# A hand-written order of tasks in a fused attention and MLP kernel: the first 220 of 1230 tasks arranged anew

## The chip, the cores and the metric

The kernel runs on one core of a Trainium2 chip. A core has five instruction queues that run side by side and meet at semaphores: PE (TensorE, matmuls, with its weight loads shown as PEld), ACT (ScalarE), DVE (VectorE), POOL (GpSimd) and SP (SyncE, which here issues nearly all transfers). The metric is the device time of one execution in microseconds, median of the runs.

## The reference, cut to what matters

One transformer layer with 2048 tokens (S), width D = 512, 32 heads of 16, and an MLP of inner width 1376. A vector c gives scale, shift and gate for both halves. Attention is linear: queries and keys go through a small matrix per head and two softmaxes of 16, and keys are summed into one matrix per head.

```python
mod = (_silu(c) @ w_mod).reshape(c.shape[0], 6, 1, -1)      # sa, ca, ga, sb, cb, gb
h = _layernorm(x, axis=-1) * (1 + ca) + sa
x = x + ga * _A_ref(h, A_wqkv, A_w_phi, A_wo)
h = _layernorm(x, axis=-1) * (1 + cb) + sb
x = x + gb * _B_ref(h, B_w_gate, B_w_up, B_w_down)
...
pq = jnp.einsum('bhsd,hdf->bhsf', q, w_phi)                 # the same for k
phi_q = jnp.concatenate([_softmax(pq, axis=-1), _softmax(-pq, axis=-1)], axis=-1)
kv = jnp.einsum('bhsf,bhsd->bhfd', phi_k, v)
o = num / den                                               # phi_q @ kv over phi_q @ sum(phi_k)
...
h = _sigmoid(g) * u                                         # MLP: g, u = x @ w_gate, x @ w_up
```

## The kernel before

The 2048 tokens are 16 tiles of 128. All work is cut into 1230 named tasks. A task has a name, the engines that may run it (the first is the default), the keys that it reads and writes, and the buffers that it uses. The function `arrange` walks a string, `ORDER`, and emits the tasks in exactly this order; each engine runs its own tasks in the order in which they stand there. A letter behind @ picks the engine (A is ACT, D is DVE, P is POOL). Buffers (8 PSUM banks, 8 tiles xn, and so on) are handed out in the same walk, so a task also waits for whoever used its buffer last. Nothing is rearranged later, and no planner runs.

The tasks up to the key features of tile 4, by name (a number behind a name is the tile, or the tile group and the block j of 128 columns):

- `ld_...` on SP: loads. `ld_x0a` to `ld_x3a` bring x, `ld_wk0` and `ld_wk1` the key weights, `ld_wm00a` to `ld_wm01b` the first part of w_mod, `ld_wv0` the value weights, `ld_wmga` the gate's part of w_mod, `ld_wmm2` its last 1.5 MB (L556), `ld_wo` the output weights. `wqT0` to `wqT3` (L669) load a block of the query weights with a DMA that transposes.
- `wdz`, `warm0`, `warm1_0` to `warm1_11` (L600): matmuls on zeros into a spare bank.
- `c1`, `c2`, `c3`: silu of c. `modc1.0`, `modc1.1` (PE, L630) and `modc1c0`, `modc1c1` (L635, L638): scale and shift of the first layer norm. `modca`: the first gate. `modc2.0`, `modc2.1` (PE, L616) and `modc2c` (ACT, L643): the second layer norm's and the second gate; they read what `ld_wmm2` brings.
- `tpw`, `wTc`: transposes of the key weights on PE and their copies out of PSUM on ACT. `fold1j` and `fold0j` (PE, L679) multiply key and query weights by the small per-head matrix; `foldc` (ACT, L685) copies the result.
- `st1_t` (DVE, L702 and L703): mean and variance of a token tile. `rs1_g`: one over the root, of tile group g, on ACT (L709, L710) or POOL (L712, L713). `nmr1_g` (DVE, L718) and `xn1_t` (POOL, L731): the normalised tile. Groups 0 and 1 are tiles 0 and 1, group 2 is tiles 2 and 3, and so on in pairs up to group 8.
- `tphgj` (PE, L744) transposes xn; tiles 10 to 13 go by DMA instead (`xT1_t`, SP, L736). `hm1_gj` puts scale and shift on it, on ACT (L751), DVE or POOL (L753).
- `Kt`, `Vt`, `Qt` (PE, L817, L821, L871): keys, values and queries of tile t; a and b are their halves. `et`, `nt`, `rt`, `phit`: the two softmaxes of the keys (exp on ACT, L776; sums on DVE, L780; reciprocal on DVE or ACT, L794 and L795; product on DVE or POOL, L787). `qe`, `qn`, `qphi`: the same for queries. `va`: values copied out of PSUM. `kv` (PE, L282): the sum over tiles.

Behind these come the rest of keys and queries, `kvn` and `kvz` (DVE, L294 and L299), which close the sum over all tiles, `num` (PE, L326), the output projection, the second layer norm and the MLP, whose matmuls `g`, `u` and `y` take most of PE's time.

In SP's queue a load is issued only when the one eight issues earlier has landed, since eight completion semaphores are used in turn.

Of the kernel before, what the change touches and what calls it, by code (L numbers as in the profile page):

```python
# [43 lines left out]
modc1c1 st1_8 ld_x3a warm1_8 K1a hm1_23 xn1_5 xn1_4 tph12 nmr1_6 st1_9 hm1_03@A hm1_13@A hm1_02@A ld_wv0 wqT3 xn1_10 xn1_11 rs1_5@P K0a K0b tph31 hm1_42@A
warm1_9 hm1_12@A hm1_22@A tph32 e0.0 K3a tph30 K3b hm1_30@A ld_wmga K1b tph33 warm1_10 tph40 st1_14 st1_15 st1_13 hm1_31@A hm1_32 wqT0 e3.0 wqT1 K2b hm1_40
nmr1_5 rs1_8@P n0.0 nmr1_8 hm1_33 e2.0 V0a V1a fold03 xn1_9 xn1_8 V1b V0b e1.0 n2.0 V2a V2b tph50 hm1_50 warm1_11 xn1_15 xn1_14 n1.0 V3a wqT2 fold00 fold01
tph43 r0.0@A va1 va0 phi0.0 foldc03 fold02 foldc01 foldc02 n3.0 st1_12 foldc00 xT1_10 xT1_11 r2.0 va2@D ld_wmm2 modca.0 modca.1 hm1_60@P hm1_63@P hm1_62@P
tph82 hm1_82@A r3.0@A modcac r1.0@A phi2.0@D phi1.0@D V3b K4a K4b rs1_7@P Q0 Q2 kv0.0 Q1 qe0.0 va3 qe2.0 hm1_43@A qe1.0 modc2.0 tph52 modc2.1 tph51 nmr1_7
xn1_12 xn1_13 phi3.0@D ld_wo qn0.0 modc2c e4.0 kv1.0 qn2.0 hm1_52 kv2.0 Q4 K5a kv3.0 xT1_12 xT1_13 qphi0.0@P qphi0.1@P qn1.0 qe4.0 qphi2.1 tph80 K5b hm1_80@A
hm1_51@A e5.0 pT0 qphi2.0 n4.0 r4.0@A qn4.0 n5.0 phi4.0@D qphi1.1@P hm1_61@P qphi1.0@P tph53 V5 K7a V4 va5 hm1_53@A V6 pT2 hm1_70@P qphi4.1 va4 hm1_71 mask4  # L50
va6 K6a K7b K6b e6.0 K8 tph83 hm1_83 r5.0 qphi4.0@P e8.0 pT1 pT4 ld_wd2 tph81 hm1_81 n6.0 n8.0 e7.0 n7.0 V7 kv4.0 hm1_72@P K11 K9 V9 K14 V8 r6.0@A e9.0 va7
# [1007 lines left out]
```

## Time and profile before

| | |
|---|---|
| three runs | 205.24, 205.37, 207.14 us; median 205.37 |
| the profiled execution | span 203.3 us from the first to the last instruction; the execution's own time is not listed apart from it |
| busy share of the span | PE 96%, DVE 79%, ACT 52%, POOL 50% |
| chain that ended last | PE 75%, DVE 8%, ACT 4%, DMA 4%, issue 4%, POOL 3% |
| instructions | 4138, of them 1447 matmuls |
| transfers | 22.94 MB in 49453 packets |

The profile is one execution, seen by the hardware profiler. Times are microseconds from the start of the span. "Busy" counts an engine's own instructions; matmul ends are modelled. The chain of waits goes back from the last instruction, at each step to what released it. In timelines, a bracket at the end of a row is the idle time before that row and what ended it. Some matmul records are missing from a trace, so a count of x3 can stand for four.

### The profile page before, as it was taken

To read this page: it belongs to the slowest core of one execution; us is meant where nothing else is said; L and a number is where in the kernel's file an instruction comes from. 1 tells how busy PE (TensorE), PEld (TensorE's weight loads), DVE (VectorE), ACT (ScalarE), POOL (GpSimd) and SP (SyncE) were. 2 spreads that over 40 slices of the span, in tenths; PEclk is the share of its full clock that TensorE was granted. 3 is DMA by queue.
4 is the path that set the end of the run, shared out by engine and by line. 5 is a ranking of instruction groups with operands and counts; after the bars stand their busy time and mean duration, and the time that the engine had idled before them with its cause. 6 is when DMAs were issued, how large, how long until landed. Compare 5 with 4: busy or idle time off the path is not lost.

```text
span 203.3 us, 4138 instructions
## 1 busy us (share of the span) xinstructions
PE 194.9 (96%) x1447; PEld 106.7 (52%) x1471; DVE 160.6 (79%) x374; ACT 105.9 (52%) x257; POOL 102.1 (50%) x143
## 2 busy tenths in 40 slices
PE   7789999999999999999999999999999999999993
PEld 2455655555464687668844444444444444444442
DVE  3899999999999999999897797794969844326633
ACT  2799999999978984556451115212113311324100
POOL 4698977789689999767670056230030324000000
PEclk9999999999999999999999999999999999999999
DMA  5999975669952792417637224433112030100111
GB/s 172 331 329 182 233 264 102 123 82 280 400 213 43 146 102 55 94 37 106 125 59 103 51 54 103 101 83 77 26 26 69 13 79 31 40 13 7 50 55 55
DMA packets 49453, 22.94 MB, mean 113 GB/s; under 512 B 38065, under 2 KB 47634, under 8 KB 49426
## 3 DMA queue, kind: packets, MB, share of 16 engines
q1 hardware_dynamic: 48896, 22.59, 48.6%
q8 instruction: 13, 0.21, 0.4%
q14 instruction: 14, 0.11, 0.2%
q10 hardware_dynamic: 530, 0.02, 0.1%
HBM read 11.58 MB, written 2.10 MB: 67 GB/s over the span
## 4 chain that ended last, share of the span: by engine, by line
PE 75%; DVE 8%; ACT 4%; DMA 4%; issue 4%; POOL 3%; SPq 0%; POOLq 0%; DVEq 0%
PE y_ps L485 19%; PE u_ps L447 18%; PE g_ps L447 17%; PE a_ps L356 5%; DMA wmod_sb<-in_w_mod_dram 4%; PE k_ps L817 3%; PE warm L600 3%; DVE ks L780 3%; PE num L326 2%; POOL phi L787 2%; PE q_ps L871 2%; PE v_ps L821 2%; PE g_ps L449 1%; ACT h1T L751 1%; DVE qks L780 1%
## 5 line engine op out<-in xcount | busy, mean ns | idle before, releaser
L457 ACT ACTIVATE tg<-g_ps 128x512 bf16<-128x512 f32 (+5 forms) x66 | 28.8, 455 | 66.7 <-PE g_ps L447 39.5
L468 DVE SCALAR_TENSOR_TENSOR wmod_sb<-tg,u_ps 128x512 bf16<-128x512 bf16 (+4 forms) x63 | 30.3, 492 | 18.0 <-ACT tg L457 11.3
L485 PE MATMUL y_ps<-wd_sb,wmod_sb 128*128 128x512 bf16 (+4 forms) x180 | 44.2, 366 | 0.2
L447 PEld LDWEIGHTS <-wg_sb 128*128 128x128 bf16 (+1 forms) x252 | 21.9, 99 | 16.1 <-issue 0.2
L447 PEld LDWEIGHTS <-wu_sb 128*128 128x128 bf16 (+1 forms) x252 | 21.8, 99 | 16.0 <-issue 0.3
L784 POOL TENSOR_TENSOR qphi<-qe,qks 128x512 bf16<-128x512 bf16 x24 | 25.1, 1063 | 3.9 <-DMA pT<-qphi 1.0
L485 PEld LDWEIGHTS <-wmod_sb 128*128 128x128 bf16 (+1 forms) x187 | 17.1, 98 | 16.0 <-issue 0.6
L447 PE MATMUL u_ps<-wT_sb,wu_sb 128*128 128x512 bf16 (+2 forms) x124 | 23.8, 322 | 0.1
L447 PE MATMUL g_ps<-wT_sb,wg_sb 128*128 128x512 bf16 (+2 forms) x122 | 23.0, 321 | 0.2
L447 PE MATMUL g_ps<-wqk_sb,wg_sb 128*128 128x128 bf16 (+4 forms) x127 | 19.9, 286 | 0.1
L447 PE MATMUL u_ps<-wqk_sb,wu_sb 128*128 128x128 bf16 (+4 forms) x127 | 19.8, 286 | 0.2
L492 DVE TENSOR_TENSOR ot<-y_ps,x 128x512 bf16<-128x512 f32 (+2 forms) x17 | 11.1, 654 | 10.5 <-PE y_ps L485 10.4
L780 DVE TENSOR_REDUCE qks<-qe 128x64 bf16<-128x1024 bf16 x16 | 19.2, 1204 | 0.0
L780 DVE TENSOR_REDUCE ks<-e 128x64 f32<-128x1024 bf16 (+2 forms) x22 | 19.1, 905 | 0.0
L376 POOL TENSOR_SCALAR ve<-mv 128x2 f32<-128x2 f32 (+1 forms) x8 | 1.8, 226 | 34.2 <-DVE mv L366 34.1
L776 ACT ACTIVATE e<-k_ps 128x512 bf16<-128x512 f32 (+2 forms) x44 | 17.7, 504 | 0.1
L776 ACT ACTIVATE qe<-q_ps 128x512 bf16<-128x512 f32 x32 | 17.3, 608 | 0.8 <-POOL phi L787 0.4
L787 POOL TENSOR_TENSOR phi<-e,kr 128x1024 bf16<-128x1024 bf16 (+2 forms) x10 | 14.5, 1454 | 3.9 <-ACT kr L795 2.1
L817 PE MATMUL k_ps<-wqk_f,h1T 128*128 128x512 bf16 x61 | 15.9, 379 | 0.1
L356 PE MATMUL a_ps<-wo_sb,oT 128*128 128x512 bf16 x60 | 15.9, 379 | 0.2
L871 PE MATMUL q_ps<-wqk_f,h1T 128*128 128x512 bf16 x60 | 15.7, 379 | 0.2
L821 PE MATMUL v_ps<-wv_sb,h1T 128*128 128x512 bf16 x62 | 15.5, 379 | 0.0
(131 smaller groups left out, 306.4 us busy)
## 6 DMA issues: line engine op xcount, KB each, us to landing
out_dram<-ot SPq DMA_DIRECT2D x15, 128.0 KB, 1.8
x_sb<-in_A_x_dram SPq DMA_DIRECT2D x6, 256.0 KB, 4.9
wmod_sb<-in_w_mod_dram SPq DMA_DIRECT2D x1, 1536.0 KB, 7.4
wu_sb<-in_B_w_up_dram SPq DMA_DIRECT2D x1, 1376.0 KB, 11.0
wg_sb<-in_B_w_gate_dram SPq DMA_DIRECT2D x1, 1376.0 KB, 10.4
wd_sb<-in_B_w_down_dram SPq DMA_DIRECT2D x1, 1280.0 KB, 8.0
wmod_sb<-in_w_mod_dram SPq DMA_DIRECT2D x4, 256.0 KB, 6.0
wqk_sb<-in_A_wqkv_dram SPq DMA_DIRECT2D x2, 256.0 KB, 4.5
```

Source lines behind the costliest of these rows:

```text
L356: pe.matmul(ap_[:], lhsT=oT[:, j, :], rhs=wo_sb[:, j, :], start=(j == 0), stop=(j == KT - 1))
L447: pe.matmul(ps[:fsz, 0:n], lhsT=w[:, j, ft * P:ft * P + fsz], rhs=h[:, j, 0:n], start=(j == 0), stop=(j == KT - 1))
L457: G.add(f"tg{k}.{ft}", {"ACT": 0.13 + n * 0.00083}, lambda e, tg=tg, g_ps=g_ps, fsz=fsz, n=n: act.activation(tg[:fsz, 0:n], g_ps[:fsz, 0:n ...
L468: dve.scalar_tensor_tensor(hm_all[:fsz, hm[k].slot, ft, 0:n], tg[:fsz, 0:n], 1.0, u_ps[:fsz, 0:n], op0=ALU.add, op1=ALU.mult)
L485: mm = pe.matmul(y[:, 0:c1 - c0], lhsT=hm_all[:fsz, hm[k].slot, ft, tl * P:(tl + 1) * P], rhs=wd_sb[:fsz, ft, c0:c1], start=(ft == 0), sto ...
L776: act.activation(ee[:, a:b, s].rearrange("p g f h -> p g (f h)"), kp[:, a * 64:b * 64].rearrange("p (g n) -> p g n", n=64), ACT.Exp, scale ...
L780: dve.tensor_reduce(ks[:, a:b].rearrange("p g s h -> p (g s) h"), ee[:, a:b].rearrange("p g s f h -> p (g s) h f"), axis=AX.X, op=ALU.add)
L784: engine(e).tensor_tensor(ph[:].rearrange("p (g s f h) -> p g s f h", s=2, f=DH, h=4)[:, :, s], ee[:, :, s], ks[:, :, 1 - s].unsqueeze(2). ...
L787: engine(e).tensor_tensor(ph[:, a * P:b * P].rearrange("p (g f h) -> p g f h", f=DH, h=4), ee[:, a:b].rearrange("p g s f h -> p (g s) f h" ...
L817: pe.matmul(kp[:], lhsT=h1T[:, j, t * P:(t + 1) * P], rhs=wqk_f[:, j, D:2 * D], start=(j == 0), stop=(j == KT - 1))
L821: pe.matmul(vp[:], lhsT=h1T[:, j, t * P:(t + 1) * P], rhs=wv_sb[:, j, :], start=(j == 0), stop=(j == KT - 1))
L871: pe.matmul(qp[:], lhsT=h1T[:, j, t * P:(t + 1) * P], rhs=wqk_f[:, j, 0:D], start=(j == 0), stop=(j == KT - 1))
```

## The change

The string ORDER begins differently: its first 220 tasks, up to the point where `e4.0` (the exponentials of tile 4's keys) follows, stand in another order. They are the same 220 tasks, and six of them change engine: `rs1_0` and `rs1_4` from ACT to POOL, `hm1_21` and `r2.0` from DVE to ACT, `modc1c1` and `hm1_12` from ACT to DVE. The other 1010 tasks stand as they did. No function is touched.

```diff
 ORDER = """
-pmem ld_x0b wdz warm0 c1 warm1_0 warm1_1 bd st1_2 st1_3 warm1_2 warm1_3 c2 rs1_2 ld_x0a ld_wk0 warm1_4 tpw0 st1_0 rs1_0 wTc0 st1_1 ld_wk1 rs1_1 c3 xn1_0
...
+wdz warm0 c1 warm1_0 warm1_1 warm1_2 warm1_3 warm1_4 ld_x0b st1_3 st1_2 rs1_2 pmem ld_x0a c2 st1_1 ld_wk0 nmr1_2 tpw1 c3 rs1_1 ld_x1b wTc1 nmr1_1 st1_0 ld_wk1
...
```

What it moves is seen in the queues of the engines. First SP, from the load of x3a to ld_wmm2 (a line with + stands only in the new order, one with - only in the old; L537 is x, L551 wv, L669 a transposing load of query weights, L555 ld_wmga, L736 the two xT1, L556 ld_wmm2):

```order
+L669 DMA_TRANSPOSE wT_sb<-in_A_wqkv_dram 128x4x128
 L537 DMA x_sb<-in_A_x_dram 128x4x512
 L551 DMA wv_sb<-in_A_wqkv_dram 128x4x512
+L669 DMA_TRANSPOSE wT_sb<-in_A_wqkv_dram 128x4x128 x2
+L555 DMA wqk_sb<-in_w_mod_dram 128x4x512
 L669 DMA_TRANSPOSE wT_sb<-in_A_wqkv_dram 128x4x128
-L555 DMA wqk_sb<-in_w_mod_dram 128x4x512
-L669 DMA_TRANSPOSE wT_sb<-in_A_wqkv_dram 128x4x128 x3
 L736 DMA_TRANSPOSE h1T<-xn 128x4x128 x2
 L556 DMA wmod_sb<-in_w_mod_dram 128x4x1536
```

One transposing load has moved ahead of x3a, two stand ahead of ld_wmga instead of one, and one is left behind it instead of three; the set of issues ahead of ld_wmm2 is the same.

Next POOL, from `bd` to the tile that the first xT1 reads. Before (L731 is xn1, L712 and L713 together one rs1; the last row's x4 are tiles 5, 4, 10 and 11):

```order
L580 TENSOR_TENSOR bd<-wp_sb,bmask 128x4x64 x2
L731 TENSOR_SCALAR xn<-x_sb,rs_84,nmr 128x512 x5
L712 TENSOR_SCALAR ve_83<-mv_82 128x2
L713 TENSOR_TENSOR rs_84<-ve_83,mhalf 128x2
L712 TENSOR_SCALAR ve_83<-mv_82 128x2
L713 TENSOR_TENSOR rs_84<-ve_83,mhalf 128x2
L731 TENSOR_SCALAR xn<-x_sb,rs_84,nmr 128x512 x4
```

Now, from the rs1_0 that follows the first two xn1 (the x4 are tiles 7, 6, 5 and 4, the x3 tiles 11, 10 and 8):

```order
L713 TENSOR_TENSOR rs_84<-ve_83,mhalf 128x1
L731 TENSOR_SCALAR xn<-x_sb,rs_84,nmr 128x512
L712 TENSOR_SCALAR ve_83<-mv_82 128x2
L713 TENSOR_TENSOR rs_84<-ve_83,mhalf 128x2
L712 TENSOR_SCALAR ve_83<-mv_82 128x2
L713 TENSOR_TENSOR rs_84<-ve_83,mhalf 128x2
L731 TENSOR_SCALAR xn<-x_sb,rs_84,nmr 128x512 x4
L712 TENSOR_SCALAR ve_83<-mv_82 128x2
L713 TENSOR_TENSOR rs_84<-ve_83,mhalf 128x2
L712 TENSOR_SCALAR ve_83<-mv_82 128x2
L713 TENSOR_TENSOR rs_84<-ve_83,mhalf 128x2
L731 TENSOR_SCALAR xn<-x_sb,rs_84,nmr 128x512 x3
```

Ahead of tiles 10 and 11, which the xT1 read, stood nine xn1 in all with themselves and two rs1; now nine xn1 and five rs1 stand there.

Last DVE, around nmr1_6 (L718), which those two xn1 need. Before, from nmr1_3 on (L753 is hm1_23, the statistics are those of tile 8):

```order
L718 TENSOR_SCALAR nmr<-mv_82,rs_84 128x1 x2
L702 BN_STATS st_81<-x_sb 128x6
L703 BN_AGGR mv_82<-st_81 128x2
L753 TENSOR_SCALAR h1T<-tp_h,modc 128x256
L718 TENSOR_SCALAR nmr<-mv_82,rs_84 128x1 x2
```

Now, from modc1c1 on (L753 in turn: hm1_12, hm1_23, and as x2 hm1_40 and hm1_33):

```order
L638 TENSOR_TENSOR modc<-modc_ps,mone 128x2x2
L753 TENSOR_SCALAR h1T<-tp_h,modc 128x128
L753 TENSOR_SCALAR h1T<-tp_h,modc 128x256
L702 BN_STATS st_81<-x_sb 128x6
L703 BN_AGGR mv_82<-st_81 128x2
L702 BN_STATS st_81<-x_sb 128x6
L703 BN_AGGR mv_82<-st_81 128x2
L753 TENSOR_SCALAR h1T<-tp_h,modc 128x256 x2
L718 TENSOR_SCALAR nmr<-mv_82,rs_84 128x1 x2
```

nmr1_6 has moved behind modc1c1, hm1_12, the second of the statistics, hm1_40 and hm1_33; the two last read what PE's tph40 and tph33 write.

On PE, the new order puts tpw1, fold11 and the transposes tph10, tph12 and tph11 early, the warm matmuls warm1_5 to warm1_11 all ahead of tph21 (before, they stood singly between transposes and keys up to V3a), and tph52 ahead of modc2.0 instead of between modc2.0 and modc2.1.

More of the change, by code (lines that the diff above doesn't have):

```diff
@@ L44 @@
[L44 to L51, printed above, removed]
@@ new lines @@
+ld_x1a bd xn1_3 warm1_5 tpw0 wTc0 fold11 warm1_6 xn1_1 tpw2 foldc11 wTc2 st1_6 tph10 tph12 st1_7 tph11 ld_wm00b rs1_0@P tpw3 warm1_7 fold10 st1_5 xn1_2 wTc3
+tph13 fold12 warm1_8 warm1_9 ld_wm00a fold13 modc1.0 foldc10 foldc12 st1_4 rs1_4@P tph20 warm1_10 warm1_11 ld_x2b foldc13 modc1c0 hm1_11@A tph21 xn1_0
+hm1_10@A rs1_3@P tph02 tph01 ld_wm01b hm1_21@A ld_wm01a hm1_01@A nmr1_4 tph23 tph00 hm1_00@A st1_11 modc1.1 xn1_7 xn1_6 st1_10 nmr1_3 xn1_5 tph22 modc1c1@D
+K1a hm1_20@A ld_x2a hm1_12 hm1_02@A wqT1 ld_x3a tph03 xn1_4 hm1_23 hm1_13@A tph41 st1_8 hm1_03@A hm1_41@A st1_9 K0a hm1_22@A rs1_6@P tph43 hm1_43@A tph40 K1b
@@ new lines @@
+rs1_5@P K0b ld_wv0 wqT3 tph30 tph33 tph32 K2a tph42 hm1_40 wqT2 fold01 hm1_33 tph31 nmr1_6 K2b ld_wmga st1_14 hm1_30@A xn1_11 e0.0 hm1_31@A wqT0 xn1_10 xT1_11
+K3a xT1_10 K3b foldc01 nmr1_5 xn1_8 V3a st1_15 e3.0 V0a rs1_8@P e2.0 V0b V3b fold03 va3 foldc03 ld_wmm2 V2a st1_12 n0.0 V2b xn1_9 fold02 nmr1_8 r0.0@A hm1_32
+modca.0 va0 foldc02 modca.1 tph50 n2.0 xn1_15 modcac hm1_50 n3.0 e1.0 xn1_14 phi0.0 hm1_60@P V1a V1b hm1_62@P K4a hm1_63@P fold00 tph82 tph52 K4b foldc00
+r2.0@A va1 va2@D r3.0@A Q0 st1_13 rs1_7@P hm1_82@A n1.0 hm1_42@A kv0.0 Q2 Q1 r1.0@A phi3.0@D phi2.0@D modc2.0 qe0.0 modc2.1 nmr1_7 qe2.0 ld_wo xn1_12 phi1.0@D
```

76 lines of the change are left out of this document (38 added, 38 removed).

## The prediction

> **What bounds the kernel now.** I read the page first (busy shares and the 40 slices), then the windows of three stretches, the chain of waits in order of time, and last the timelines of PE (the matmul engine), SP (the queue that issues transfers), POOL, DVE and ACT in the first 60 us. The windows give, for each stretch, its length and the busy time of PE, weight load, DVE, ACT and POOL, then granted clock, DMA share and GB/s:
>
> ```profile
> 6.40:28.90 22.50, 20.11 (x194) 11.98 (x194) 21.45 (x60) 21.74 (x59) 18.30 (x29) 1.00 1.16 280
> 28.90:58.20 29.30, 29.09 (x284) 16.36 (x288) 28.49 (x51) 28.03 (x80) 23.26 (x22) 1.00 0.76 203
> 76.00:200.00 124.00, 123.26 (x766) 65.12 (x778) 90.13 (x203) 38.48 (x80) 39.57 (x56) 1.00 0.29 60
> ```
>
> PE is full (29.09 of 29.30, 123.26 of 124.00) from 28.9 us on, apart from short waits between 58 and 76. Whatever the front gains, PE must hand it on at 28.9. Before 28.9 PE idles 22.50 - 20.11 = 2.39 us: this is the only place where the changed tasks (they end at about 29 us) can save PE time. The chain of waits says what stands at 28.9 (start, length, what):
>
> ```profile
> 20.76 0.59 SPq L736
> 21.36 0.05 issue
> 21.41 7.44 DMA wmod_sb<-in_w_mod_dram
> 28.85 0.05 issue
> 28.90 0.82 PE modc_ps L616 x24
> ```
>
> The 1.5 MB load ld_wmm2 is issued at 21.41, lands at 28.85, and the matmuls of modc2.0 start at 28.90. In the timeline of PE the bracket at the end of a row is the idle time before it and what ended it:
>
> ```profile
> 8.92 0.62 PE L679 MATMUL fold_ps<-bd,wT_sb 128*128 128x128 bf16 x8 [0.94 <-ACT wT_sb L664]
> 28.90 0.82 PE L616 MATMUL modc_ps<-sc_bf,wmod_sb 128*128 128x1 bf16 x24 [0.22 <-DMA wmod_sb<-in_w_mod_dram]
> 29.58 0.27 PE L744 MATMUL tp_h<-ident,xn 128*128 128x128 bf16 x2
> 29.69 0.81 PE L616 MATMUL modc_ps<-sc_bf,wmod_sb 128*128 128x1 bf16 x24
> 58.57 0.93 PE L326 MATMUL num<-kvb,pT 128*128 128x68 bf16 x24 [0.36 <-DVE kvb L299]
> ```
>
> PE had come to modc2.0 only 0.22 us before the load landed. So two things meet at 28.9: PE's own work and one transfer. Whoever comes later sets the rest, since modc2.0 blocks all that is queued behind it on PE (kv1.0, kv2.0, Q4, K5a), and modc2c blocks ACT behind it (e4.0).
>
> **The change part by part.** Its size is the smaller of what PE and the transfer gain.
>
> PE's arrival. No matmul is added or removed; the order of 220 tasks changes. The largest hole, 0.94 us before fold11, came from ACT, which did rs1_0 and rs1_1 between the copies wTc. Now rs1_0 and rs1_4 run on POOL, tpw1 and wTc1 come first, and seven single warm matmuls (warm1_5 to warm1_11) stand in the early holes instead of among the transposes. If no idle time were left, PE would come to modc2.0 at 28.90 - 2.39 + 0.11 = 26.6 us; 0.11 is tph52, now ahead of modc2.0 (29.58 to 29.69 above). Some waits stay. The first copy wTc ran here on ACT:
>
> ```profile
> 6.89 0.59 ACT L664 COPY wT_sb<-tp_w 128x512 bf16<-128x512 bf16 x1 [0.24 <-PE tp_w L661]
> ```
>
> Now it is wTc1, and fold11 can't start before it ends at 7.48, while PE has only tpw1, one warm matmul and tpw0 before that: some 0.4 us idle. I allow 0.2 more for modc1.1, which needs its load and a PSUM bank from hm1_21. So about 27.2, and PE is 1.7 us early.
>
> ACT and DVE. The rows for the six changes of engine (start, length):
>
> ```profile
> 6.12 0.30 ACT L709 ACTIVATE ve<-mv,eps 128x1 f32<-128x1 f32 x1 [0.20 <-DVE mv L703]
> 6.45 0.20 ACT L710 ACTIVATE rs<-ve 128x1 f32<-128x1 f32 x1
> 12.19 2.42 ACT L751 ACTIVATE h1T<-tp_h,modc 128x128 bf16<-128x128 bf16 x6
> 14.48 0.18 ACT L635 COPY modc<-modc_ps 128x2 f32<-128x2 f32 x1
> 14.77 2.42 ACT L751 ACTIVATE h1T<-tp_h,modc 128x128 bf16<-128x128 bf16 x6
> 30.72 1.17 ACT L776 ACTIVATE e<-k_ps 128x512 bf16<-128x512 f32 x2
> 13.34 0.40 DVE L753 TENSOR_SCALAR h1T<-tp_h,modc 128x256 bf16<-128x256 bf16 x1
> 25.93 0.52 DVE L798 RECIPROCAL kr<-ks 128x64 bf16<-128x64 f32 x1
> ```
>
> ACT loses two rs1 (0.50 each by 0.30 + 0.20), modc1c1 (0.29 from 14.48 to 14.77) and hm1_12 (about 0.38, six from 12.19 to 14.48); it takes hm1_21 (0.38) and r2.0 (about 0.5). Net 1.0 + 0.29 + 0.38 - 0.38 - 0.5 = 0.8 us less. DVE loses hm1_21 (0.40) and r2.0 (0.52), takes hm1_12 and modc1c1 (at most 0.40 and 0.29): 0.2 us or more saved. Both are busy for nearly all of 6.4 to 28.9 (21.74 and 21.45 of 22.50), so they reach the end of the changed part some 0.6 us earlier. This is cover, not gain: e4.0 started at 30.72, behind modc2c, which needs modc2.1, which needs the load.
>
> The load. So the sum hangs on when ld_wmm2 lands. SP's timeline before:
>
> ```profile
> 9.42 1.01 SPq L551 DMA_DIRECT2D wv_sb<-in_A_wqkv_dram  x1
> 10.47 1.78 SPq L669 DMA_TRANSPOSE wT_sb<-in_A_wqkv_dram  x1
> 12.30 0.58 SPq L555 DMA_DIRECT2D wqk_sb<-in_w_mod_dram  x1
> 12.92 5.08 SPq L669 DMA_TRANSPOSE wT_sb<-in_A_wqkv_dram  x3
> 18.12 3.23 SPq L736 DMA_TRANSPOSE h1T<-xn  x2
> 21.41 0.57 SPq L556 DMA_DIRECT2D wmod_sb<-in_w_mod_dram  x1
> ```
>
> From 9.42 SP issues with hardly a gap up to 21.41, and the same 21 issues stand ahead of ld_wmm2 in both orders (15 loads, 4 wqT, xT1_10 and xT1_11). Only their order differs: wqT1 goes between x2a and x3a, wqT3 and wqT2 behind wv0, ld_wmga follows them, then wqT0, xT1_11, xT1_10. If each issue keeps its length, ld_wmm2 is issued at 21.4 and lands at 28.85. How the new order changes that no row shows, so I bound the shift.
>
> Earliest: the two xT1 need xn1_11 and xn1_10 from POOL.
>
> ```profile
> 5.24 1.50 POOL L580 TENSOR_TENSOR bd<-wp_sb,bmask 128x256 bf16<-128x256 bf16 x2 [2.13 <-DMA wp_sb<-in_A_w_phi_dram]
> 8.57 3.95 POOL L731 TENSOR_SCALAR xn<-x_sb,rs,nmr 128x512 bf16<-128x512 bf16 x5 [1.83 <-ACT rs L710]
> 14.54 3.03 POOL L731 TENSOR_SCALAR xn<-x_sb,rs,nmr 128x512 bf16<-128x512 bf16 x4
> 17.54 0.22 POOL L712 TENSOR_SCALAR ve<-mv 128x2 f32<-128x2 f32 x1
> 18.53 0.22 POOL L712 TENSOR_SCALAR ve<-mv 128x2 f32<-128x2 f32 x1
> ```
>
> Nine xn and two rs1 stood ahead, done at 14.54 + 3.03 = 17.57. Now nine xn and five rs1 do: three more at 18.53 - 17.54 = 0.99 are 2.97 us. But POOL can start its first xn when bd ends at 6.74, not at 8.57, if the statistics of tiles 3 and 2 come first (they do): 17.57 + 2.97 - 1.83 = 18.7. One issue of half 3.23 us after that, ld_wmm2 could go at 20.3, 1.1 us earlier.
>
> Latest: DMA throughput around transposes, from the windows of one us (last numbers: DMA share, GB/s):
>
> ```profile
> 17.00:18.00 1.00, 1.00 (x9) 0.54 (x7) 0.97 (x4) 1.00 (x3) 0.92 (x3) 1.00 1.15 349
> 18.00:19.00 1.00, 1.00 (x10) 0.56 (x8) 0.88 (x3) 1.00 (x4) 0.92 (x3) 1.00 2.93 103
> 19.00:20.00 1.00, 1.00 (x8) 0.44 (x5) 0.84 (x4) 1.00 (x4) 0.55 (x2) 1.00 0.27 52
> ```
>
> From 349 GB/s the queue falls to 103 and 52 where the transposes behind ld_wmga begin: (246 + 297) / 349 = 1.6 us of load time lost. The new order has three groups of transposes among the loads instead of two, so up to 1.6 us later.
>
> I take 0 between -1.1 and +1.6: the transfers ahead are the same ones, and the row of before (21.41) is the nearest. [...]
>
> Sum: landing 0, PE's work behind modc2.0 less tph52 -0.11, hence -0.1 us. PE then waits some 1.7 us instead of 0.22: its early gain is paid back at one point. The 0.36 us before num at 58.57 is DVE's; DVE's lead would cut it only if PE, which feeds it from 28.9 on, were earlier too. The profiled execution spans 203.3 us; the median of the runs is 205.37, so 2.1 us lie around the span, and they stay. 203.2 + 2.1, or 205.37 - 0.1: **205.3 us**.
>
> **The rivals.**
> A, the load comes early: with transposes spread among loads SP no longer issues five in a row (12.92 to 21.35 but for gaps), and POOL allows 1.1 us. For it: DMA fell to 52 GB/s while SP was still issuing. Against: each of SP's transposes was long exactly there, which a new order repeats. Midway, 0.7 earlier: 205.37 - 0.7 - 0.1 = 204.6; at the bound 204.2.
>
> B, slower: wqT1 between x2a and x3a costs its own dip in the queue, ld_wmga, wqT0 and the xT1 land later, and so does ld_wmm2; PE stands at L616 for longer. It decides from a landing after 28.96 (28.85 + 0.11). Middle of 0.4 to 1.6, 1.0 later: 205.37 + 1.0 - 0.1 = 206.3.
>
> C, slower by another way: nmr1_6 on DVE now stands behind hm1_40 and hm1_33, whose transposes tph40 and tph33 stand on PE behind K0a and K0b, which need ACT's hm1_03. POOL wants nmr1_6 for xn1_11 at 18.7 less two xn (3.03 / 4 = 0.76 each), 17.2. DVE's rows of one statistic:
>
> ```profile
> 15.34 0.68 DVE L702 BATCH_NORM_STATS2 st<-x_sb 128x6 f32<-128x512 bf16 x1
> 16.15 0.66 DVE L702 BATCH_NORM_STATS2 st<-x_sb 128x6 f32<-128x512 bf16 x1
> ```
>
> If modc1c1 starts at 13.6 (14.48 before, less ACT's lead of some 0.9), then with 0.29 for it, four hm1 at 0.40 and two statistics at 0.81 nmr1_6 starts at 17.1: just in time. What is late here goes one for one into xn1_11, both xT1 and ld_wmm2. At 0.8: 206.1.
>
> D, the clock: PE pauses at modc2.0. At the start the matmuls, though the granted clock reads full, ran at half the later rate:
>
> ```profile
> 1.24 2.74 PE L600 MATMUL warm<-wd_sb 128*128 128x512 bf16 x6 [1.24 <-DVE wd_sb L593]
> 36.21 2.32 PE L817 MATMUL k_ps<-wqk_f,h1T 128*128 128x512 bf16 x10
> ```
>
> 2.74 / 6 = 0.46 against 2.32 / 10 = 0.23 us each. If the pause of 1.7 us brought that state back for the 5.2 us that it lasted at the start (11 warm matmuls, 1.24 to tpw0), half would be lost: 2.6, total 207.9. The longest pause of before, 0.94 us, can't test it. [...]
>
> **How the numbers follow.** Forecast 0.47, A 0.22, B 0.20, C 0.07, D 0.04. The range 204.3 to 206.7 leaves out D, the far end of A (0.07) and of B and C (0.05): 0.16. One per cent, about what a measurement of this kernel can tell from no change, is 2.05 us: below 203.3 is only a load earlier than its bound (0.04); above 207.4 is D and a B worse than its bound (0.07); the rest, 0.89, is within.
>
> **What would show it.** In the changed profile: modc2.0 (L616, x24) waiting for DMA wmod_sb for 1 to 2 us; ld_wmm2 (L556) issued between 20.3 and 23.0 and landing near 28.9; the hole of 0.94 before fold11 gone; first xn on POOL near 6.8; PE full from there to num near 58.5. PE reaching modc2.0 after the load, or a landing off by over 1.6 us, would make the prediction wrong.

## The result and the profile after

| | before | changed |
|---|---|---|
| median of the runs | 205.39 us (204.68 to 207.56, 14 runs) | 203.90 us (203.60 to 204.34, 14 runs) |
| span of the profiled execution | 203.3 us | 202.3 us |
| runs with a mean granted clock under 0.995 | 23 of 35 (the runs beside e1, e2, e3 and e6 below) | 0 of 14 |

The ratio changed to before is 0.9911 [0.9888, 0.9934]: 0.9% faster, 1.5 us by the medians. In a second comparison (e7 below) the medians are 1.6 us apart, and the mean spans of the runs at full clock 1.4 us (203.33 and 201.97). The forecast was 205.3 with a range from 204.3; the result lies below it. The windows of the changed kernel over the same stretches (length, then busy time of PE, weight load, DVE, ACT and POOL, granted clock, DMA share, GB/s):

```profile
6.40:28.90 22.50, 20.84 (x244) 12.74 (x241) 21.31 (x60) 22.24 (x57) 20.97 (x33) 1.00 1.13 284
28.90:58.20 29.30, 28.77 (x261) 15.55 (x259) 29.05 (x57) 27.99 (x82) 24.04 (x23) 1.00 0.78 195
```

Before 28.9 PE now idles 22.50 - 20.84 = 1.66 us, where it idled 2.39. After 28.9 it idles 0.53 instead of 0.21: a little of the gain is given back. The chain of waits of the changed kernel, its pieces around ld_wmm2:

```profile
17.62 1.82 POOL xn L731 x3
20.52 6.87 DMA wmod_sb<-in_w_mod_dram
27.43 1.49 PE modc_ps L616 x48
```

The load is issued at 20.52 and lands at 27.39; before it was 21.41 and 28.85. The load is 1.46 us earlier, and modc2.0 starts 1.47 us earlier. The timeline of SP says how the issue came earlier (start, length); the two xT1 stand last, one by one, first those of before and then the changed kernel's:

```profile
8.72 1.50 SPq L669 DMA_TRANSPOSE wT_sb<-in_A_wqkv_dram  x1
11.44 2.95 SPq L669 DMA_TRANSPOSE wT_sb<-in_A_wqkv_dram  x2
15.06 1.57 SPq L669 DMA_TRANSPOSE wT_sb<-in_A_wqkv_dram  x1
17.96 2.50 SPq L736 DMA_TRANSPOSE h1T<-xn  x2
20.52 0.74 SPq L556 DMA_DIRECT2D wmod_sb<-in_w_mod_dram  x1
...
18.12 1.92 SPq L736 DMA_TRANSPOSE h1T<-xn  x1
20.14 1.22 SPq L736 DMA_TRANSPOSE h1T<-xn  x1
...
17.96 1.19 SPq L736 DMA_TRANSPOSE h1T<-xn  x1
19.25 1.21 SPq L736 DMA_TRANSPOSE h1T<-xn  x1
```

The same six transposing issues that took 1.78 + 5.08 + 3.23 = 10.09 us before now take 1.50 + 2.95 + 1.57 + 2.50 = 8.52. SP is done with the four wqT at 16.63 instead of 18.00, but then stands 1.33 us until POOL has written tile 11, so the first xT1 is issued only 0.16 us earlier (17.96 instead of 18.12). The other 0.73 us of the 0.89 are the pair of xT1 itself, 2.50 instead of 3.23. The rows of PE that matter, and one each of DVE, ACT and POOL:

```profile
7.31 0.40 PE L679 MATMUL fold_ps<-bd,wT_sb 128*128 128x128 bf16 x4 [0.44 <-ACT wT_sb L664]
12.66 0.55 PE L630 MATMUL modc_ps<-sc_bf,wmod_sb 128*128 128x1 bf16 x16 [0.56 <-DMA wmod_sb<-in_w_mod_dram]
24.30 1.02 PE L871 MATMUL q_ps<-wqk_f,h1T 128*128 128x512 bf16 x4 [0.36 <-ACT wqk_f L685]
27.43 1.49 PE L616 MATMUL modc_ps<-sc_bf,wmod_sb 128*128 128x1 bf16 x48
36.89 0.39 PE L744 MATMUL tp_h<-ident,xn 128*128 128x128 bf16 x4
37.45 1.02 PE L821 MATMUL v_ps<-wv_sb,h1T 128*128 128x512 bf16 x4 [0.17 <-ACT vaug L836]
57.51 0.93 PE L326 MATMUL num<-kvb,pT 128*128 128x68 bf16 x24 [0.36 <-DVE kvb L299]
...
28.00 0.33 DVE L718 TENSOR_SCALAR nmr<-mv,rs 128x1 f32<-128x1 f32 x2 [0.60 <-POOL rs L713]
...
29.93 1.18 ACT L776 ACTIVATE e<-k_ps 128x512 bf16<-128x512 f32 x2
...
17.17 2.27 POOL L731 TENSOR_SCALAR xn<-x_sb,rs,nmr 128x512 bf16<-128x512 bf16 x3
```

modc2.0 has no bracket (idle times under 0.15 us get none): PE and the load came together again, at 27.4. Behind it the V matmuls come at 37.45 where an unbroken PE would come at 37.12 (36.89 + 0.23, as 38.36 to 38.59 before): 0.33 us is lost there to ACT. In e7's profile, the same kernel once more, modc2.0 starts at 27.16, PE waits 0.22 us for DVE at 29.00, and the V matmuls come at 37.46, again behind ACT: the lead is not handed on in full. So num, 58.57 before, is 1.06 us earlier and not 1.47, and so is the end of the span (203.3 to 202.3).

### The profile page after: what moved, and what is told of

Its sections match the earlier page's. It is cut to its first block, busy times and chain, and to the rows that moved or that the text cites. A ratio compares the mean times of both kernels' runs of the same rounds, so it can differ in the third digit from the quotient of the medians.

```text
span 202.3 us, 4156 instructions
## 1 busy us (share of the span) xinstructions
PE 195.3 (97%) x1471; PEld 106.1 (52%) x1471; DVE 160.1 (79%) x374; ACT 105.1 (52%) x253; POOL 104.7 (52%) x147
## 4 chain that ended last, share of the span: by engine, by line
PE 74%; DVE 7%; DMA 6%; ACT 5%; SPq 3%; issue 2%; POOL 1%; POOLq 0%; DVEq 0%; ACTq 0%
PE y_ps L485 19%; PE u_ps L447 18%; PE g_ps L447 17%; DMA wmod_sb<-in_w_mod_dram 6%; PE a_ps L356 6%; PE k_ps L817 3%; PE v_ps L821 3%; PE num L326 2%; PE q_ps L871 2%; ACT e L776 2%; DVE ks L780 2%; PE g_ps L449 1%; DVE qks L780 1%; SPq L537 1%; DVE phi L787 1%
## 5 line engine op out<-in xcount | busy, mean ns | idle before, releaser
L457 ACT ACTIVATE tg<-g_ps 128x512 bf16<-128x512 f32 (+5 forms) x66 | 28.9, 455 | 66.8 <-PE g_ps L447 39.7
L485 PE MATMUL y_ps<-wd_sb,wmod_sb 128*128 128x512 bf16 (+4 forms) x187 | 45.7, 367 | 0.0
L817 PE MATMUL k_ps<-wqk_f,h1T 128*128 128x512 bf16 x64 | 16.6, 379 | 0.0
```

The costliest lines, as they stand in the source:

```text
L457: G.add(f"tg{k}.{ft}", {"ACT": 0.13 + n * 0.00083}, lambda e, tg=tg, g_ps=g_ps, fsz=fsz, n=n: act.activation(tg[:fsz, 0:n], g_ps[:fsz, 0:n ...
L485: mm = pe.matmul(y[:, 0:c1 - c0], lhsT=hm_all[:fsz, hm[k].slot, ft, tl * P:(tl + 1) * P], rhs=wd_sb[:fsz, ft, c0:c1], start=(ft == 0), sto ...
L817: pe.matmul(kp[:], lhsT=h1T[:, j, t * P:(t + 1) * P], rhs=wqk_f[:, j, D:2 * D], start=(j == 0), stop=(j == KT - 1))
```

## The experiments

In the edits a line with + or - names tasks of ORDER; the rest of the string is as in the kernel named. Each run lists its mean granted clock. One stretch of 3.41 us at half clock (0.50, as in e3's and e8's windows below) in a span of 203 us makes 1 - 3.41 x 0.5 / 203 = 0.992, two make 0.983. All runs fall near 0.983, near 0.991, or from 0.996 to 1.0; under 0.995 is called low.

| kernel | median us | ratio to before [95%] | low clock | mean span of the other runs |
|---|---|---|---|---|
| before, four comparisons | 205.37 to 205.74 | | 58 of 93 | 203.33 to 203.53 |
| changed (the result above; e7) | 203.90; 203.76 | 0.9911 [0.9888, 0.9934]; 0.9905 [0.9867, 0.9943] | 0 of 20 | 202.15; 201.97 |
| e1, changed, issue order of before | 204.69 | 0.9963 [0.9936, 0.9991] | 3 of 12 | 202.76 |
| e2, before, new issue order | 205.40 | 1.0000 [0.9972, 1.0027] | 10 of 12 | 202.90 |
| e3, changed, load ahead of the xT1 | 206.93 | 1.0058 [1.0029, 1.0086] | 7 of 12 | 204.52 |
| e6, changed, engines of before | 205.10 | 0.9963 [0.9938, 0.9988] | 3 of 12 | 203.23 |
| e8, changed without the seven warm | 205.25 | 0.9977 [0.9949, 1.0006] | 10 of 12 | 202.50 |
| e9, before, early warm | 205.42 (205.30 without its longest run, 207.85) | 0.9994 [0.9963, 1.0026] | 2 of 12 | 203.54 |
| e10, before, early warm and new issue order | 204.39 | 0.9933 [0.9906, 0.9960] | 2 of 12 | 202.57 |
| e5, changed, nmr1_7 later | 203.54 | 0.9878 [0.9839, 0.9917] | 1 of 7 | 201.68 |
| e11, changed, three moves | 204.43 | 0.9945 [0.9918, 0.9971] | 2 of 12 | 202.69 |
| e12, e5 and two more warm | 203.69 | 0.9919 [0.9893, 0.9945] | 0 of 8 | 202.01 |

**e1: the changed kernel with the issues in the old order.** The folds on PE are permuted so that each finds its block of weights.

```diff
 SP, from ld_x2a on
-ld_x2a wqT1 ld_x3a ld_wv0 wqT3 wqT2 ld_wmga wqT0 xT1_11 xT1_10 ld_wmm2 ld_wo
+ld_x2a ld_x3a ld_wv0 wqT3 ld_wmga wqT0 wqT1 wqT2 xT1_10 xT1_11 ld_wmm2 ld_wo
 PE (foldc on ACT likewise)
-fold01 ... V3b fold03 ... V2b fold02 ... tph50 ... fold00
+fold03 ... V3b        ... V2b fold00 ... tph50 fold01 ... fold02
```

> The changed kernel, with the twelve issues on SP from the load x2a to the load wo in the order of before (the three weight transposes wqT0, wqT1, wqT2 behind ld_wmga, wqT3 behind ld_wv0), and the four query folds on PE permuted so that each finds its transpose landed. Theory 1 (both needed: modc2.0 starts at the later of PE's arrival and the landing of ld_wmm2): ld_wmm2 is issued near 21.4 again and lands near 28.9, PE comes near 27.4 and waits about 1.5 us, and the time is 205.2, within 0.4. Theory 2 (the gain is PE's and ACT's earlier front alone): 203.9, as the changed kernel, even with such a wait. Theory 3 (the gain is the earlier load alone): 205.4, as before. Theories 1 and 3 part in the next run.

204.69: 0.8 to 0.9 us of the gain went, 0.7 stayed, so none of the three numbers. At full clock the spans say the same: 202.76 on average, 0.6 over the changed kernel's 202.15 and 0.8 under the 203.53 of before. The profiled execution had a stretch at half clock; e1b is a second profile of the same kernel.

> The kernel of run e1 (changed, with the issue order of before) once more, for a profile with the clock at 1.0 throughout, since e1's had a stretch at half clock. Theory 1 (modc2.0 starts at the later of PE's arrival and the load): ld_wmm2 issued near 21.3, landed near 28.6, PE at modc2.0 near 27.4 and waiting 1.2 us, and a span near 203.2, which leaves the 0.7 us by which e1 beat the kernel before unexplained. Rival: the load lands earlier here than in the kernel before, near 28.1, because something ahead of it on SP or in the queue is shorter, and the span is near 202.7.

Its span is 202.5. PE, SP and POOL there, at full clock throughout (POOL's x3 are tiles 11, 10 and 8):

```profile
28.30 1.50 PE L616 MATMUL modc_ps<-sc_bf,wmod_sb 128*128 128x1 bf16 x48 [0.49 <-DMA wmod_sb<-in_w_mod_dram]
...
12.91 5.09 SPq L669 DMA_TRANSPOSE wT_sb<-in_A_wqkv_dram  x3
18.62 2.70 SPq L736 DMA_TRANSPOSE h1T<-xn  x2
21.37 0.58 SPq L556 DMA_DIRECT2D wmod_sb<-in_w_mod_dram  x1
...
17.07 2.28 POOL L731 TENSOR_SCALAR xn<-x_sb,rs,nmr 128x512 bf16<-128x512 bf16 x3
```

With the old issue order the issue is back at 21.37 (21.41 before, 20.52 changed), and PE waits for the load, as theory 1 has it. But the load takes 28.25 - 21.37 = 6.88 us, as in the changed kernel (6.87) and not as before (7.44). The rival of e1b holds: of the 1.46 us by which the landing moved, 0.89 are the issue and go with the order of the twelve issues; 0.57 are the flight and do not. The 0.6 us that modc2.0 stays ahead of before (28.90 - 28.30) is most of what e1 keeps. Which part of the order gives the issue is seen in the rows: SP is done with the wqT at 18.00 and waits 0.62 us, since xT1_10, first in the old order, reads tile 10, which POOL writes second, at 18.59 (17.07 and two of 0.76). The pair of xT1 starts 0.66 us later than in the changed kernel and takes 0.20 longer. What the wqT spread among the loads give without the exchange of the two xT1 no run shows.

**e2: the kernel before with the new issue order only.** The edit is the first one of e1, in the other direction, on the kernel before.

> The kernel before, with only the twelve issues on SP from the load x2a to the load wo in the order of the changed kernel; PE, ACT, DVE and POOL as before. Theory 1 (both needed): ld_wmm2 is issued at 20.5 or earlier and lands by 27.4, PE comes at 28.7 as before and finds it there, so only the wait of 0.22 us goes: 205.2. Theory 2 (PE's front alone): 205.4. Theory 3 (the earlier load alone): 203.9.

205.40, no gain, as theories 1 and 2 have it within the interval; theory 3 (the earlier load alone) falls. In ten of twelve runs the clock was low, and then PE comes later still. In the profiled one PE reached L616 at 29.11, with the load issued at 19.93. The two runs at full clock span 202.8 and 203.0 us, under each of the twelve such runs of before beside them (203.1 to 204.6). So the earlier load alone probably gives some 0.6 us, which the clock hides in the median; two runs are few for it.

**e3: the load ahead of both xT1.**

```diff
 SP
-wqT0 xT1_11 xT1_10 ld_wmm2 ld_wo
+wqT0 ld_wmm2 xT1_11 xT1_10 ld_wo
```

> The changed kernel, with ld_wmm2 issued ahead of the two transposes xT1_11 and xT1_10, in the 1.33 us that SP waited there for POOL. Theory 1 (PE's own work now sets modc2.0 at 27.4): the load is issued near 16.7 and lands near 24, modc2.0 starts no earlier than 27.2, and the time is 203.8, within 0.3; both xT land later, behind the load, which may hold hm1_60 on POOL, and with it rs1_7, by up to 1 us and cost up to 0.5 us. Theory 3 (the load alone sets modc2.0): modc2.0 starts at 25 or earlier and the time is under 202.5.

206.93, slower. modc2.0 started at 27.36, so PE's own work sets it and the earlier load gains nothing; that part of theory 1 held. The price of the late xT1 was far over the 0.5 us allowed. POOL, DVE and PE of e3:

```profile
27.45 1.63 POOL L753 TENSOR_SCALAR h1T<-h1T,modc 128x256 bf16<-128x256 bf16 x3 [2.83 <-DMA h1T<-xn]
...
30.09 0.34 DVE L718 TENSOR_SCALAR nmr<-mv,rs 128x1 f32<-128x1 f32 x2 [2.60 <-POOL rs L713]
...
31.08 1.04 PE L282 MATMUL kvacc<-vaug,phi 128*128 128x68 bf16 x16 [2.08 <-DVE phi L787]
```

The 1.5 MB load, issued at 17.00, took 9.3 us to land (6.9 in the changed kernel), and of the two transposes issued behind it, from 18.02 on, one took 7.89 (the four of the changed kernel took 2.4 to 4.6). hm1_60 on POOL waited 2.83 us for them, rs1_7 behind it kept nmr1_7 on DVE for 2.60, phi1.0 stood behind that, and kv1.0 on PE for 2.08. Three engines, one late tile. At full clock the spans average 204.52, 2.4 us over the changed kernel. In the profiled execution the clock then halved, as e3's windows show:

```profile
27.76:31.17 3.41, 1.33 (x44) 1.16 (x42) 1.08 (x4) 2.71 (x9) 2.90 (x6) 1.00 0.18 53
31.17:34.59 3.42, 3.20 (x23) 1.77 (x24) 3.42 (x4) 1.70 (x4) 3.27 (x4) 0.50 0.32 61
```

**e6: the six changes of engine undone**, in the changed order.

```diff
-rs1_0@P rs1_4@P modc1c1@D hm1_12 hm1_21@A r2.0@A
+rs1_0 rs1_4 modc1c1 hm1_12@A hm1_21 r2.0
```

> The changed kernel's order with the six changes of engine undone (rs1_0, rs1_4, modc1c1 and hm1_12 on ACT; hm1_21 and r2.0 on DVE). Theory 1: ACT has 0.8 us more to do in the front and PE comes later by 0.3 to 0.8 us; POOL has two rs1 fewer, so xn1_11 and the load come earlier and PE's work alone sets modc2.0: 204.2 to 204.7. A rival, that the order alone did it and the engines' changes are cover: 203.9 or below.

205.10, worse than either theory. Among runs that are not low it is 203.23 - 202.06 = 1.2 us over the changed kernel (202.06 is the mean of its two means). So the changes of engine belong to the gain: this order needs them. How the 1.2 us come about at full clock stays open, since the profiled execution had half clock from 13.82 to 17.24. The load was not earlier there: it was issued at 22.13. DVE and SP of e6:

```profile
17.95 0.41 DVE L753 TENSOR_SCALAR h1T<-tp_h,modc 128x256 bf16<-128x256 bf16 x1 [1.02 <-PE tp_h L744]
18.27 0.33 DVE L718 TENSOR_SCALAR nmr<-mv,rs 128x1 f32<-128x1 f32 x2
...
15.04 1.58 SPq L669 DMA_TRANSPOSE wT_sb<-in_A_wqkv_dram  x1
19.57 2.50 SPq L736 DMA_TRANSPOSE h1T<-xn  x2
```

With PE at half clock its transposes come late, hm1_33 on DVE waits 1.02 us for them, nmr1_6 stands behind it (18.27; 16.34 in the changed kernel), POOL writes tile 11 late, and SP stands from 16.62 to 19.57. This is the chain that the prediction named as rival C. It is there in all five profiles of the changed front with half clock in this place: the first xT1 is issued at 19.96 in e1, 19.87 in e8, 19.20 in e5 and 19.48 in e11, against 17.96. PE itself is late too: in e6 the load lands at 28.91 and modc2.0 follows at 29.08 without a bracket.

**e7, e8: is the clock part of the gain?** e7 is the changed kernel itself, beside e8 to e10. e8 drops its seven single warm matmuls, whose results go nowhere.

```diff
-for i in range(12):  warm(f"warm1_{i}", ...)
+for i in range(5):   warm(f"warm1_{i}", ...)
 PE
-... warm1_5 ... warm1_6 ... warm1_7 ... warm1_8 warm1_9 ... warm1_10 warm1_11 ...
```

> The changed kernel as it is, beside the next three on one chip. The clock theory (the granted clock halves for a stretch of 3.4 us wherever a 3.4 us stretch before it holds too few streamed matmul columns; this happened in 23 of 35 runs of the kernel before in the first comparison and in none of 14 of the changed one): 203.9, a mean granted clock of 0.997 or more in at least 9 of 12 runs. Rival, that the granted clock depends on the chip and the hour: as many runs under 0.995 here as of the kernel before, and 204.5 or more.

> The changed kernel without the seven single warm matmuls warm1_5 to warm1_11 (their results go nowhere), so that the early holes on PE stay empty. The clock theory: most runs show a mean granted clock near 0.99, a stretch of 3.4 us at half clock between 9 and 17 us costs 0.8 to 1.7 us of PE's work, and PE comes to modc2.0 after the load: 204.8 to 205.4. Rival, that seven fillers in holes do nothing for the time: 203.7 to 204.0, and the clock stays at 1.0.

e7: 203.76, no low run of six, where 19 of 29 runs of before beside it are low. e8: 205.25, low in ten of twelve. The clock theory holds in both numbers: without the seven matmuls the median is 1.5 us longer. Its two runs at full clock span 202.4 and 202.6. e8's windows (the granted clock is the last column but two):

```profile
8.89:12.30 3.41, 2.33 (x37) 1.41 (x34) 3.27 (x11) 3.38 (x10) 2.89 (x7) 1.00 1.16 311
12.30:15.71 3.41, 2.91 (x28) 1.81 (x29) 3.27 (x11) 3.16 (x9) 3.33 (x6) 0.50 1.21 273
```

PE's timeline of e8 in the first of these windows, and ahead of modc2.0:

```profile
8.91 0.40 PE L679 MATMUL fold_ps<-bd,wT_sb 128*128 128x128 bf16 x4
9.47 0.40 PE L679 MATMUL fold_ps<-bd,wT_sb 128*128 128x128 bf16 x4 [0.16 <-ACT wT_sb L664]
10.27 0.55 PE L630 MATMUL modc_ps<-sc_bf,wmod_sb 128*128 128x1 bf16 x16 [0.40 <-DMA wmod_sb<-in_w_mod_dram]
10.68 0.38 PE L744 MATMUL tp_h<-ident,xn 128*128 128x128 bf16 x4
11.42 0.79 PE L744 MATMUL tp_h<-ident,xn 128*128 128x128 bf16 x5 [0.35 <-DVE xn L729]
...
28.18 1.89 PE L871 MATMUL q_ps<-wqk_f,h1T 128*128 128x512 bf16 x8
29.91 1.24 PE L616 MATMUL modc_ps<-sc_bf,wmod_sb 128*128 128x1 bf16 x40
```

Busy time does not part the stretches that half clock follows from the others: 2.33 us of PE here are followed by half clock, 2.12 us in one window of the kernel before were not. Columns do, in these profiles. Eight matmuls of 512 columns follow each other in 29.91 - 28.18 = 1.73 us, 0.42 ns a column. From 8.89 to 12.30 there are 17 matmuls of 128 columns and 16 of one: 17 x 128 x 0.42 ns = 0.92 us, 0.27 of the stretch. The same sum for every stretch of 3.41 us between 5 and 35 us, in the fourteen profiles. The stretches are counted in steps of the 3.41 us that half clock lasts, from the moments at which the trace notes a change of clock; that the steps run on where no change is noted is assumed (in the traces of before and of the changed kernel two changes lie 197.97 us apart, 58 steps of 3.413):

| share by columns (at full clock) | profile | the next 3.41 us |
|---|---|---|
| 0.06; 0.27; 0.32; 0.32; 0.33; 0.34; 0.37 | e3; e8; e2; e11; e5; e1; e6 | half clock, each |
| 0.41; 0.41; 0.41; 0.42; 0.42 | before (10.29); e3; e10; before (27.36); before (6.88) | full clock, each |
| 0.47; 0.48; 0.48; 0.48; 0.54 (the lowest of each) | changed; e7; e9; e12; e1b | full clock, each |

The border lies between 0.37 and 0.41 in these profiles; it is read from the same profiles, and no other measure of PE's work than busy time was compared. Stretches that are at half clock themselves are left out, and near the border they do not part clearly: e8's from 12.30 holds 0.38 by the same sum and is followed by half clock, e2's from 11.77 holds 0.35 to 0.39 (as matmuls on its edges are counted) and is followed by full. Where the 3.41 us begin differs between the profiles (a change is noted at 6.88 in the profile before, at 5.87 in the changed one). That the same kernel is low in only some of its runs for this reason is the author's estimate, from these profiles: with the steps slid along the profile before, at least one step between 3.5 and 30 us has under 0.39 for 77% of the possible beginnings (62% of its runs were low: 58 of 93). For the changed kernel it is 15% (none of 20), for e8 some 75 to 83% (10 of 12), for e2 some 75 to 86% (10 of 12), for e12 0 to 6% (none of 8), by where the border is put; for e6 it is some 48% (3 of 12). So it is a rough guide.

**e9, e10: the two parts put into the kernel before.** e9 moves its seven warm matmuls alone, e10 also the issues as in e2.

```diff
 PE
+warm1_5 warm1_6 warm1_7 (ahead of fold11)   warm1_8 (ahead of fold12)
+warm1_9 warm1_10 (behind modc1.0)           warm1_11 (ahead of modc1.1)
-warm1_5 to warm1_11 (behind tph22 and later)
```

> The kernel before, with the seven warm matmuls alone moved into the holes before fold11, before fold12 and around modc1.0 and modc1.1; every other engine and SP as before. The clock theory: the clock stays at 1.0 in most runs. Theory 1 (modc2.0 starts at the later of PE's arrival and the load): PE comes 0.9 us earlier (four of the matmuls stood where PE was full, 0.22 us each) and waits for the load, which lands near 28.8 as before: 205.1. Rival, that PE's front alone sets the time: 204.4.

> The kernel before, with the seven warm matmuls moved as in the run before and the twelve issues on SP in the changed kernel's order; ACT, DVE and POOL as before. Theory 1: the load lands near 27.4 or earlier, PE comes near 27.9, nothing waits: 204.3, so that these two parts give about 1.1 of the 1.5 us. Rival, that the six changes of engine and the new order of ACT, DVE and POOL are what gives the gain: 205.1.

205.42 and 204.39. By the medians neither part alone gives anything, both together 1.0 us. The two parts do two things, which the medians do not part: they bring PE and the load earlier, and they keep the clock up (2 of 12 runs low, against 19 of 29 of before beside them). At full clock alone the spans of e10 are 0.8 us under those of before (202.57 and 203.33), e9's 0.2 over. PE and the chain of waits of e9, then PE and SP of e10:

```profile
29.60 0.82 PE L616 MATMUL modc_ps<-sc_bf,wmod_sb 128*128 128x1 bf16 x24 [0.50 <-DMA wmod_sb<-in_w_mod_dram]
```

```profile
22.19 7.36 DMA wmod_sb<-in_w_mod_dram
```

```profile
28.24 0.82 PE L616 MATMUL modc_ps<-sc_bf,wmod_sb 128*128 128x1 bf16 x24
...
20.11 0.58 SPq L556 DMA_DIRECT2D wmod_sb<-in_w_mod_dram  x1
```

e9's clock is full and its PE early, but it waits for the load, which SP issues in the old order. (In this execution SP runs some 0.8 us behind the profile of before from its eleventh issue on, and the span is 204.3, where e9's full-clock runs average 203.54; so the size of the wait may be this execution's.) In e10 the load is issued 1.30 us earlier than before and no wait is left at modc2.0. By the trace's completion events it lands at 28.19, 8.08 us after its issue and later than the 27.4 expected, so PE and the load meet once more, at 28.2. The 0.6 us from e10 to the changed kernel (204.39 to 203.76) belong to the rest: the new order of ACT, DVE and POOL with the changes of engine, by which PE comes to modc2.0 at 27.43 and not at 28.24.

**e5, e11, e12: what is still to be had.** e5 takes away DVE's wait at nmr1_7; e11 adds two moves; e12 puts two more warm matmuls into the hole of 0.56 us ahead of modc1.1.

```diff
 e5
-nmr1_7 ... xn1_12 phi1.0@D
+phi1.0@D nmr1_7 xn1_12
 e11, and e5
-K4a fold00 (PE)   e1.0 foldc00 (ACT)   rs1_5@P xn1_11 xn1_10 xn1_8 (POOL)   nmr1_5 st1_15 (DVE)
+fold00 K4a        foldc00 e1.0         xn1_11 xn1_10 rs1_5@P xn1_8          st1_15 nmr1_5
 e12, and e5
+warm1_12 (PE, two matmuls, ahead of modc1.1)
```

> The changed kernel, with nmr1_7 on DVE moved behind phi1.0 (and xn1_12 on POOL with it in the list). In the changed kernel DVE waited 0.60 us at nmr1_7 for rs1_7 on POOL, with phi1.0 and all behind it queued, and PE gave back 0.33 us between 36.9 and 37.5, at the V matmuls that wait for ACT's vaug. Theory: DVE comes 0.5 us earlier to qn0.0, PE's loss there goes, and the time is 0.2 to 0.4 below the changed kernel's: 203.5. Rival, that ACT's own work sets vaug there and DVE's lead changes nothing: 203.85.

> The changed kernel with three moves: nmr1_7 as in the run before; V1a, V1b and fold00 ahead of K4a on PE and foldc00 ahead of e1.0 on ACT, so that Q0 no longer waits 0.36 us for foldc00; rs1_5 on POOL behind xn1_11 and xn1_10, with nmr1_5 and xn1_8 behind it, so that SP issues both xT1 and ld_wmm2 about 0.5 us earlier. Theory 1 (PE's arrival and the load both set modc2.0, now both near 27.0): 0.4 less at modc2.0 and 0.3 less at V5: 203.2. Rival, that one of the two moves fails to bring its side earlier (the load by its place in the queue, or PE by a wait of K4a): 203.5, as the run before.

> The kernel of run e5 with one more warm task of two matmuls (results go nowhere) ahead of modc1.1 on PE, in the hole of 0.56 us in which PE waits for the load of wm01. In e5's profile the stretch of 3.41 us ahead of the half-clock stretch held matmuls for 0.33 of its time by columns, and no stretch with 0.41 or more was followed by half clock in any profile so far; two matmuls of 0.215 us raise it to 0.45. The clock theory: no run has a mean granted clock under 0.995 (e5: one of 7), and DVE's wait at nmr1_7 is gone as in e5: 203.5 or 0.1 less, PE without idle time at the V matmuls near 37.5. Rival, that the clock falls with single idle gaps and not with what a stretch of 3.41 us holds: one or two of 12 runs fall as before.

e5: 203.54, and 0.3 to 0.5 us under the changed kernel in the spans of the runs that are not low. The two were not timed side by side, and e12, which has the same move, averages 202.01 at full clock, as the changed kernel does (202.15 and 201.97). So a gain in time is not shown. That the wait itself goes is seen in e12, which has the same move and a profile at full clock. DVE and PE of e12 (its line numbers from 605 on are one higher):

```profile
27.90 0.34 DVE L719 TENSOR_SCALAR nmr<-mv,rs 128x1 f32<-128x1 f32 x2
...
36.80 0.39 PE L745 MATMUL tp_h<-ident,xn 128*128 128x128 bf16 x4
37.03 0.81 PE L822 MATMUL v_ps<-wv_sb,h1T 128*128 128x512 bf16 x3
57.01 0.93 PE L326 MATMUL num<-kvb,pT 128*128 128x68 bf16 x24 [0.36 <-DVE kvb L299]
```

nmr1_7 waits no more, the V matmuls follow 0.23 us after the transposes, and num comes at 57.01, 0.50 us before the changed kernel's, though modc2.0 starts at 27.4 in both. e12's median, 203.69, is not below e5's. The clock was full in all its eight runs; e5 had one low run in seven, too few to tell the two apart.

e11: 204.43, a miss. With rs1_5 moved back on POOL, DVE and PE wait, as two rows of e11 show:

```profile
21.21 0.33 DVE L718 TENSOR_SCALAR nmr<-mv,rs 128x1 f32<-128x1 f32 x2 [1.19 <-POOL rs L713]
...
24.17 0.23 PE L744 MATMUL tp_h<-ident,xn 128*128 128x128 bf16 x1 [0.54 <-POOL xn L731]
```

This execution had half clock from 13.42 to 16.84, and with such a stretch SP issued the first xT1 at 19.20 to 19.96 in e1, e5, e6 and e8 too, without this move, so how much of these waits is the move's is not shown. At full clock e11's spans average 202.69, 1.0 us over e5's.

## Why the prediction was wrong

The step that failed is the load: "I take 0 between -1.1 and +1.6: the transfers ahead are the same ones, and the row of before (21.41) is the nearest." It was -1.46 us, beyond even the lower bound: -0.89 from the issue, which the sum took to keep its lengths, and -0.57 from the flight, for which the sum had no term.

- **The issue.** "If each issue keeps its length, ld_wmm2 is issued at 21.4." The lengths did not keep: six transposing issues went from 10.09 to 8.52 us. Read one issue at a time, the trace of before shows that the lengths differ: the row of 5.08 us is 2.46, 1.27 and 1.26, and the pair of xT1 is 1.92 and 1.22. In the two profiles each wqT right behind a load took 1.50 to 2.46 us and each behind another wqT 1.26 or 1.27; but the first xT1 of before took 1.92 behind a wqT, so the place behind a load is not the whole of it. What came through is the pair of xT1 (0.73 us); the wqT's 1.37 us met POOL's tile 11 and gave 0.16. So the bound from POOL, 20.3, was nearly met (20.52). e1 and e1b show that the order of the twelve issues does it, the exchange of the two xT1 included: put back, it gives 21.37 again.
- **The flight.** It was taken to stay at 7.44 us; it was 6.87. e1b has 6.88 with the old order of the twelve issues, so that order is not what shortened it. In all nine profiles with the changed front and the load in its old place (changed, e1, e1b, e5 to e8, e11, e12) it is 6.58 to 7.03 us, in the four with the order of before on ACT, DVE and POOL (before, e2, e9, e10) 7.13 to 8.08. So it goes with the rest of the new order; how is open.
- **PE's arrival.** "About 27.2": modc2.0 started at 27.43 without a bracket, right. The hole before fold11 was 0.44 (some 0.4 foretold); the one before modc1.1 was 0.56, for which 0.2 was allowed. Since PE was early, the load's shift came through in full, where the forecast had PE wait 1.7 us.
- **ACT and DVE.** ACT's 0.8 us held: e4.0 came at 29.93 instead of 30.72. DVE's lead was eaten by the wait of 0.60 us at nmr1_7, so qn0.0 came only 0.10 us earlier (28.85), and PE lost 0.33 us at 37.45. The step "cover, not gain" held only while the load was late: once modc2.0 came 1.47 us earlier, ACT's side set the V matmuls (37.45) and the gain at num was 1.06. In e12's profile that loss is gone with the wait.
- **POOL.** Tile 10 was to be ready at 18.7; the second of three xn from 17.17, at 0.76 each, put it at 18.7.
- **Rivals.** A had the right direction and, for the issue, a bound that held (0.89 of 1.1 us); the flight took the load past it. At -1.46 in place of -1.1 its price would have been 203.8, by the sum's own arithmetic. B did not come: DMA fell to 52 GB/s between 17 and 18 us here too, but the load landed early. C did not come in the changed kernel, where nmr1_6 ran at 16.34, before the 17.2 that POOL needed; at half clock it came (e6 above). The 0.36 us before num stayed, as foretold.
- **D, the clock.** Half clock came (0.50 in e3's and e8's windows), but it was looked for in the wrong kernel. The forecast asked whether the changed kernel's pause would halve the clock; instead 58 of 93 runs of the kernel before had a low clock, and the seven warm matmuls that the change moves into the holes keep it up (e8 without them: 10 of 12 low; e9, the kernel before with them early: 2 of 12). The feared pause did not come either: PE idled 0.14 us at modc2.0. What a pause of 1.7 us there does to the clock no run shows, so D's 2.6 us and its 0.04 were the author's estimates. (The trace of before notes its first clock at 6.88 us, so the full clock read for the first matmuls there was no reading.) The profile of before was of an execution without such a stretch, and the three times, which scatter from 205.24 to 207.14, were not explained.
- **The sum's frame.** "2.1 us lie around the span" took a profiled execution for a typical one. For the changed kernel the profiled run took 204.01 with a span of 202.3, 1.7 around it. With that, the profiled execution of before took about 205.0, and the median of 205.4 stands 0.4 higher, since most runs have a half-clock stretch or a longer span than the profiled one's. So the gain is 1.5 to 1.6 us by the medians, 1.4 by the spans at full clock (203.33 and 201.97), and 1.0 by the two profiles; the clock accounts for some 0.2 us of the medians' gain directly.

## What to carry to other kernels

Where PE and a transfer arrive together, moving either alone can show nothing in the medians (e2 and e9: 0.0 us each) while moving both shows most of it (e10: 1.0 of 1.6 us), so a nearly even pair must be costed as a pair. Here the granted clock hid part of it: ten of e2's twelve runs were low, and its two at full clock were 0.6 us ahead. A shift in a queue is not zero because the queue holds the same transfers: here an issue's length changed with its place (the pair of xT1 took 3.23 us before and 2.50 in the changed kernel), so the bound ought to cover the shortest lengths that the profile shows for its kind, and the flight behind it (7.44 and 6.87 us) needs a bound of its own. And where a kernel's times scatter while its profile looks clean, look at the granted clock of each run before explaining a median by one profile.
